# Words to convert on ScalarE's DMA queue, and other wire times in the scheduler of the first stage

## The chip, the cores and the metric

The kernel runs on one core of a Trainium2 chip. A core has five engines with queues of their own: TensorE (PE, matmuls), VectorE (DVE), ScalarE (ACT), GpSimd (POOL) and SyncE (SP), which here only issues DMAs. ACT and POOL can issue DMAs too. The metric is the device time of one execution in microseconds; 1666.36 us is the median of three runs before the change.

## The reference

Attention over keys and values that are averaged over groups of eight, and behind it two layers of two matrix products each. Shapes: 8 batches, 8 heads, 576 positions, head size 64; both layers go from 512 to 2048 and back over 4608 tokens.

```
k_p = k.reshape(B, H, Sp, 8, D).mean(axis=3)         # Sp = 72, v alike
scores = scale * np.matmul(q, k_p.transpose(0, 1, 3, 2))
attn = softmax(scores)                                # minus the row maximum
x = np.matmul(attn, v_p) ...reshape(4608, 512)
h = np.maximum(x @ w_in, 0.0);   x = (h * h) @ w_out  # first layer
h = x @ w_in2;  return np.maximum(0.01 * h, h) @ w_out2
```

The four weight matrices reach the core as 8-byte floats; the kernel converts them itself.

## The kernel before

Products of 4-byte floats are made of two rounded parts: a high and a low part of each operand, and three matmuls (high by high, high by low, low by high). The work falls into stages. The first, up to about 591 us, holds the attention and the first matrix product of layer one; the middle one forms the second product of layer one from seven products of quarter matrices (class `Middle`, matmuls L1752); the last does layer two (L1970, L2213).

**The first stage.** Tokens go in nine blocks of 512. For each block: q is loaded (L212) and turned, scored against pooled keys (L749), made to probabilities (ACT L771), turned again (L829, L837), split to `pth`, `ptl`, `ptr` (ACT L843, DVE L846) and multiplied with values (L890 to L893), giving `xh` and `xl` (L902, L906). Units of 12 matmuls follow (L1021), squared after a relu (ACT L1032, L1035) and stored by POOL's queue (L1051). For each batch the K rows (L176, 1024 KB into `wo4`) and a tail of 64 rows (L163, into `raw`) are pooled by DVE (L507, L589), and the V rows (L183, 1024 KB into `wo5`) with a remainder of six loads of 32 rows (L193, into `wo2`).

**Conversions.** In the same stage 38 jobs convert the weights that later stages need. A job's words (512 KB, in one or two DMAs, L346, into `wo0` or `wo1`) are loaded; ACT takes the exponent (L243), DVE puts the bits together (L247 to L264, L1535), and POOL's queue stores the parts into `w1o`, `w2i`, `w2o`.

**The order.** The first 117 us are written out by hand. From there `FirstStage` adds every operation to a `Plan` with an engine, an estimated duration, a rank, what it comes after and which buffers it takes. `Plan.run` picks whichever can start first by its own account, ties by rank, and emits instructions in that order: an engine's program is what the account made of it, and the engine executes it in order. The account has a `wire` for loads: each transfer that has a wire time lengthens it, an SP operation isn't planned before `wire - QUEUED`, and what reads the data is planned no sooner than `lag` behind the issue, or the end of the wire and 2.0. SP's account runs 15 us (`AHEAD`) ahead of the others.

**The stage's end.** `add_second_stage` (L1596) loads weights of the middle stage from `w1o`: eight `wo` tiles (384 KB) and eight `wi` tiles (512 KB), L1719. Loads of `wo0`, `wo1`, `wo3` come after everything of attention and conversion; `wi4` to `wi7` come after units of the last block, whose weight buffers they take. ACT and DVE split each (L1725, L1727), and TensorE starts with `wo0`.

Of the kernel before, what the change touches and what calls it, by code (L numbers as in the profile page):

```python
# [16 lines left out]
P = 128  # L17
POOL = 8
# [25 lines left out]
def attention_relu2_leaky_kernel(  # L44
# [12 lines left out]
    nc = tc.nc  # L57
# [3 lines left out]
    SP = S // POOL  # L61
    PAIR = 2 * SP
    NP = H // 2
    KEYS = H * SP
# [79 lines left out]
    def load_to(key, fn, tag, shape=(P, 512)):  # L144
        t = sb(list(shape), F32, tag)
        fn(t)
        raws[key] = t
# [11 lines left out]
    def k_load(b, c):  # L159
        n = min(P, KEYS - c * P)  # L160

        def fn(t):
            nc.sync.dma_start(out=t[:n], in_=rows_of(k, b)[c * P : c * P + n])  # L163

        return fn
# [145 lines left out]
    class Weights:  # L311
# [5 lines left out]
        def load(self, n):  # L317
            self.steps[n][0]()
# [10 lines left out]
    class Stored:  # L329
# [8 lines left out]
            self.steps = self.run(range(self.at, end), val, sums)  # L338
            self.at = end

        def load(self, h, t=None):
            w, kind, _, i, n = self.jobs[h]
            if t is None:
                t = sb([P, 512, 2], U32, "val")
            for src, to in half_words_of(w, kind, i, n):
                nc.sync.dma_start(out=to(t), in_=src)  # L346
            return t[:, :, 0], t[:, :, 1]

        def run(self, jobs, val_tag, sums_tag):
# [843 lines left out]
    class Plan:  # L1193
# [1 line left out]


        SLACK = {"PE": 1.5, "ACT": 0.3, "DVE": 0.3, "SP": 0.3, "POOL": 0.3}
        AHEAD, QUEUED = 15.0, 5.0

        def __init__(self, counts):  # L1200
            self.ops, self.counts, self.rings, self.wire = [], counts, {}, -self.AHEAD
# [70 lines left out]
    class FirstStage:  # L1272

        STORED, VALUES, CHAIN, POOLING, SUMS, UNITS = 9, 0, 1, 3, 4, 6
        STORED_AT, STORED_EVERY = 30.0, 10.5

        def __init__(self):
            counts = {"ps": 4, "acc": 4, "pt": 1, "prem": 3, "x0": 1, "x1": 1, "placed": 1}
# [9 lines left out]
            self.last.append(x)  # L1288
            return x

        def dma(self, fn, rank, kb, n=1, rate=260.0, **k):
            return self.op("SP", 0.35 * n, fn, rank, lag=4.0, wire=kb / rate, **k)

        def out(self, fn, rank, kb, n=1, **k):
            return self.op("POOL", 0.8 * n, fn, rank, lag=6.0, wire=kb / 350.0, **k)

        def add_keys(self, b, rank):
            rows, tail, kp, km, kl, kt = (
                Buffer(t) for t in ("wo4", "raw", "kp", "gh", "km", "kt")
            )  # L1300
            load = self.dma(
                lambda: load_to(("k", b, "rows"), k_load_all(b), "wo4", (P, 4, 512)),
                rank, 1024, gets=[rows])
            load_tail = self.dma(
                lambda: load_to(("k", b, "tail"), k_load(b, KEYS // P), "raw"), rank, 128, gets=[tail])
            steps = []
            x = load
            for n, us in enumerate((1.22, 0.69, 0.43)):
                def fn(n=n):
                    if n == 0:  # L1310
                        steps.extend(k_pool_rows(b))
                    steps[n]()
                after = [x, self.scored.get(b - 2)] if n == 0 else [x]
                x = self.op("DVE", us, fn, rank, after=after, gets=[kp] if n == 0 else (), uses=[rows, kp])
            y = self.op("DVE", 1.03, lambda: k_pool_tail(b), rank, after=[load_tail, x], uses=[tail, kp])
            masks = []

            def mask(n):
                if n == 0:
                    masks.extend(k_mask_parts(b))  # L1320
                masks[n]()

            x = self.op("DVE", 0.68, lambda: mask(0), rank, after=[x, y], gets=[km, kl], uses=[kp])
            y = self.op("DVE", 0.28, lambda: mask(1), rank, after=[x, y], uses=[kp, kl])
            parts = []

            def turn(n):
                if n == 0:
                    parts.extend(k_transpose_parts(b))
                parts[n]()  # L1330

            p0, p1 = Buffer("ps"), Buffer("ps")
            t0 = self.op("PE", 0.63, lambda: turn(0), rank, after=[x, y], gets=[p0, kt], uses=[km])
            c0 = self.op("DVE", 0.69, lambda: turn(1), self.CHAIN, after=[t0], uses=[p0, kt])
            t1 = self.op("PE", 0.2, lambda: turn(2), rank, after=[y, t0], gets=[p1], uses=[kl])
            c1 = self.op("DVE", 0.22, lambda: turn(3), self.CHAIN, after=[t1, c0], uses=[p1, kt])
            self.keys[b] = [c0, c1], kt

        def add_v(self, b, rank):
            rows, rem, vp, vr, vh, rh = (  # L1340
                Buffer(t) for t in ("wo5", "wo2", "vp", "vr", "vh", "rh")
            )
            x = self.dma(
                lambda: load_to(("v", b, "rows"), v_load_all(b), "wo5", (P, 4, 512)),
                rank, 1024, gets=[rows])
            y = self.dma(
                lambda: load_to(("rem", b, "rows"), rem_load_all(b), "wo2", (P, 2, 512)),
                rank, 384, n=6, gets=[rem])
            steps = {}

            def pool(what, n):
                if n == 0:
                    steps[what] = (v_pool_rows if what == "v" else rem_pool_rows)(b)
                steps[what][n]()

            for n, us in enumerate((1.22, 0.69, 0.43)):
                x = self.op("DVE", us, lambda n=n: pool("v", n), rank, after=[x],
                            gets=[vp] if n == 0 else (), uses=[rows, vp])
            for n, us in enumerate((0.69, 0.42, 0.29)):
                y = self.op("DVE", us, lambda n=n: pool("r", n), rank, after=[y],  # L1360
                            gets=[vr] if n == 0 else (), uses=[rem, vr])

            def split(n):
                if n == 0:
                    steps["s"] = v_split_parts(b)
                steps["s"][n]()

            a = self.op("DVE", 0.72, lambda: split(0), rank, after=[x, y], gets=[vh, rh], uses=[vp])
            c = self.op("DVE", 0.5, lambda: split(1), rank, after=[a], uses=[vr, rh])
            c = self.op("DVE", 0.63, lambda: split(2), rank, after=[c], uses=[vr, rh])  # L1370
            self.vs[b] = [a, c], [vp, vr, vh]
# [23 lines left out]
        def add_attention(self, blk):  # L1395
# [3 lines left out]
            tiles = list(range(t0 // P, (t0 + T) // P))  # L1399
# [5 lines left out]
            for i in tiles:  # L1405
                for b, *_ in parts_of(i):
                    if b not in keyed:
# [1 line left out]
                        self.add_keys(b, self.POOLING)  # L1409
                two = len(parts_of(i)) - 1  # L1410
                raw, qt, ps = Buffer("raw"), Buffer("qt"), Buffer("ps")
                x = self.dma(lambda i=i: load_to(("q", i), q_load(i), "raw"), self.POOLING, 256,
                             n=1 + two, rate=130.0, gets=[raw])
                qp = q_transpose_parts(i)

                def copy(i=i, fn=qp[1]):
# [57 lines left out]
        def add_unit(self, blk, c, n):  # L1474
# [16 lines left out]
            x = self.plan.op("ACT", 0.6, powers, self.VALUES, after=[x], gets=[r], uses=[acc])  # L1491
            x = self.plan.op("ACT", 0.63, lambda: square(at["r"]), 2, after=[x], uses=[r])
            steps = store_parts(blk, c, lambda: at["r"], nc.gpsimd)
            y = self.plan.op("POOL", 0.8, steps[0], 0, after=[x], uses=[r], lag=4.0, wire=0.73)
            if len(steps) > 1:
                total = Buffer("gh" if blk else "wo3")
                x = self.plan.op("DVE", 0.69 if blk else 0.42, steps[1], self.SUMS,
                                 after=[x, self.even], gets=[total], uses=[r, self.even_r])
                self.plan.op("POOL", 0.8, steps[2], 0, after=[x], uses=[total], lag=4.0, wire=0.73)
            self.even, self.even_r = y, r  # L1500

        def add_stored(self, jobs):
            words, before = {}, None
            for h in jobs:
# [7 lines left out]
                def run(fn, st=st):  # L1512
                    return lambda: fn(st)

                def load(st, h=h, i=i, n=n, tiles=tiles):
                    if n == 0:
                        tiles[0] = sb([P, 2, 512, 2], U32, f"wo{i % 2}")
                    st["low"], st["top"] = stored.load(h, tiles[0][:, n])

                first = x = self.dma(run(load), R, 512, n=1 + kind, gets=[val] if n == 0 else (),  # L1520
                             uses=[val], behind=first if n else None)
                x.ready = self.STORED_AT + h * self.STORED_EVERY
                x = self.op("ACT", 0.67, run(lambda st: exponent(st["top"])), R, after=[x], uses=[val])

# [13 lines left out]
                to = forms[name][i]  # L1538
                if kind == 0 and n == 0:
                    y = self.out(run(lambda st, to=to: stored.first_half(st["o"], to, nc.gpsimd)()),  # L1540
                                 R, 128, after=[x], uses=[gl])
                    before = st, gl, x
                    continue
                sums, steps = Buffer("wo3"), []
# [10 lines left out]

                more = [] if kind else [before[1]]
                after = [x] if kind else [x, before[2]]
                x = self.out(run(begin), R, 192 if kind else 256, n=2, after=after, uses=[gl, *more])
                x = self.op("DVE", 1.0 if kind else 0.84, step, R, behind=x, gets=[sums], uses=[gl, *more])
                if not kind:  # L1560
                    x = self.op("DVE", 0.84, step, R, after=[x], uses=[sums, gl, *more])
                y = self.out(step, R, 256 if kind else 512, after=[x], uses=[sums])
            self.stored_last = y

        def run(self):
# [763 lines left out]
```

## Time and profile before

| | us |
|---|---|
| median of three runs (1665.43 to 1667.23) | 1666.36 |
| the profiled execution | 1666.54 |
| its span on the core | 1664.8 |
| PE busy in it | 1617.9 (97%) |
| DVE busy | 1268.0 (76%) |
| ACT busy | 835.2 (50%) |
| POOL busy | 170.5 (10%) |

An engine's busy time is what its instructions cover; issuing DMAs is not counted. A wait is the idle time of an engine just before an instruction, with what released it. The granted clock of TensorE (PEclk) is a share of its full speed; half of it is 1.2 GHz. DMA share is the mean busy share of 16 DMA engines.

### The profile page before, as it was taken

What the parts mean: (1) busy time and instruction counts of PE and PEld (TensorE: products, weight loads), DVE (VectorE), ACT (ScalarE), POOL (GpSimd) and SP (SyncE); (2) the same over time, 40 slices, a digit from 0 to 9 for tenths busy, and PEclk for the clock granted to TensorE, in tenths of its full rate; (3) what the DMA queues carried; (4) which work ended last, traced back from release to release, by engine and by line L of the source; (5) the groups of instructions that cost most, each with busy time, mean ns of one, the idle gap of its engine ahead of it and who ended that gap; (6) DMA issues with size and microseconds to landing.
All of it is one profiled execution on the core that took longest, in us unless ns stands there. A gap on an engine that the chain in (4) does not pass through costs nothing. (4 is left out here: it accounts for less than half of the span.)

```text
span 1664.8 us, 26658 instructions
## 1 busy us (share of the span) xinstructions
PE 1617.9 (97%) x9560; PEld 1471.1 (88%) x9560; DVE 1268.0 (76%) x2214; ACT 835.2 (50%) x1797; POOL 170.5 (10%) x289
## 2 busy tenths in 40 slices
PE   7997998999999999999999999999999999999998
PEld 6886787788888888888888899999999999999998
DVE  7986697888775578786968978877877876666665
ACT  6764576666755654443435544443445533333332
POOL 0111322233334310000000000000000000000000
PEclk9999999999999999999999999999999999999999
DMA  8846577676557877575757856556638754444443
GB/s 233 272 147 185 187 230 211 203 233 231 202 208 248 286 252 260 184 259 189 252 186 258 290 201 231 176 197 226 197 139 291 234 180 156 154 158 152 152 155 105
DMA packets 249700, 345.78 MB, mean 208 GB/s; under 512 B 55360, under 2 KB 175168, under 8 KB 249568
## 3 DMA queue, kind: packets, MB, share of 16 engines
q1 hardware_dynamic: 228704, 278.92, 52.2%
q0 software_dynamic: 20288, 64.64, 10.6%
q8 instruction: 75, 1.23, 0.3%
q10 hardware_dynamic: 576, 0.52, 0.1%
q14 instruction: 57, 0.47, 0.1%
HBM read 208.74 MB, written 135.27 MB: 207 GB/s over the span
## 5 line engine op out<-in xcount | busy, mean ns | idle before, releaser
L1021 PE MATMUL acc<-xh,wi 128*128 128x512 f32 x640 | 219.0, 400 | 0.0
L1021 PE MATMUL acc<-wo,wi 128*128 128x512 f32 x704 | 197.3, 407 | 5.5 <-ACT r L1032 5.4
L1021 PEld LDWEIGHTS acc<-wo,wi 128*128 128x128 f32 x704 | 132.4, 193 | 32.7 <-ACT r L1032 6.8
L1021 PEld LDWEIGHTS acc<-xh,wi 128*128 128x128 f32 x640 | 120.2, 188 | 23.8 <-ACT wi L303 0.2
L1021 PE MATMUL acc<-xl,wi 128*128 128x512 f32 x320 | 125.1, 391 | 0.0
L2213 PE MATMUL ps<-wi,hh 128*128 128x256 f32 x512 | 93.9, 283 | 0.0
L2213 PE MATMUL acc<-wi,hh 128*128 128x256 f32 x496 | 91.1, 283 | 0.0
L2213 PE MATMUL ps<-wo,hh 128*128 128x256 f32 x496 | 90.9, 283 | 0.0
L2213 PE MATMUL acc<-wo,hh 128*128 128x256 f32 x484 | 88.8, 283 | 0.0
L1707 ACT CAST mh<-ms 128x512 fp32r<-128x512 f32 (+2 forms) x68 | 52.4, 771 | 72.2 <-DVE ms L1689 72.0
L771 ACT ACTIVATE s<-ps,m 128x72 f32<-128x72 f32 x240 | 73.8, 330 | 29.4 <-DVE m L759 29.3
L1970 PE MATMUL acc<-fh,wo 128*128 128x384 f32 x384 | 82.9, 338 | 2.7 <-DVE gh L1983 1.6
L1970 PE MATMUL ps<-fh,wi 128*128 128x384 f32 x384 | 82.3, 336 | 0.2 <-DVE gh L1983 0.2
L1986 ACT ACTIVATE gh<-gh 128x384 f32<-128x384 f32 x48 | 25.3, 527 | 112.0 <-DVE gh L1983 112.0
L2213 PEld LDWEIGHTS ps<-wi,hh 128*128 128x128 f32 x512 | 79.9, 192 | 0.0
L2213 PEld LDWEIGHTS acc<-wi,hh 128*128 128x128 f32 x496 | 77.4, 192 | 0.0
L2213 PEld LDWEIGHTS ps<-wo,hh 128*128 128x128 f32 x496 | 77.4, 192 | 0.0
L1752 PE MATMUL acc<-mh,wi 128*128 128x512 f32 (+1 forms) x256 | 76.0, 363 | 0.0
L1752 PE MATMUL ps<-mh,wi 128*128 128x512 f32 (+1 forms) x256 | 76.0, 363 | 0.0
L2213 PEld LDWEIGHTS acc<-wo,hh 128*128 128x128 f32 x484 | 75.5, 192 | 0.0
L1032 ACT ACTIVATE r<-acc 128x512 f32<-128x512 f32 x88 | 52.5, 604 | 44.0 <-PE acc L1021 42.6
L2213 PE MATMUL ps<-wi,hl 128*128 128x256 f32 x256 | 72.4, 283 | 0.0
(359 smaller groups left out, 4518.0 us busy)
## 6 DMA issues: line engine op xcount, KB each, us to landing
h<-r POOLq DMA_DIRECT2D x88, 256.0 KB, 3.7
hf<-r SPq DMA_DIRECT2D x96, 192.0 KB
ml<-h SPq DMA_DIRECT2D x34, 512.0 KB
ml<-h SPq DMA_DIRECT2D x60, 256.0 KB
hr<-hf SPq DMA_DIRECT2D x23, 640.0 KB
xl<-hf SPq DMA_DIRECT2D x23, 640.0 KB
xh<-hf SPq DMA_DIRECT2D x23, 640.0 KB
h<-st POOLq DMA_DIRECT2D x56, 256.0 KB, 4.0
```

What stands on the lines that cost most here:

```text
L771: nc.scalar.activation(out=s[:, g, :], in_=at["ps"][:, h * SP : (h + 1) * SP], func=AF.Exp, bias=m[:, g : g + 1], accum_out=l[:, g : g + 1],)
L1021: nc.tensor.matmul(acc_of[blk, c], lhsT=(wih, wil)[w][c][:, kc], rhs=xsplit[blk][x][kc], start=(kc, n) == order[0], stop=(kc, n) == order[-1],
L1032: nc.scalar.activation(out=r, in_=ps, func=AF.Relu)
L1707: nc.scalar.copy(hi[:, at], y)
L1752: nc.tensor.matmul(at[s][:, :n], lhsT=w[:, wx, b, s * P : (s + 1) * P], rhs=x[:, a], start=p == 0 and m == 0, stop=p == PAIRS - 1 and m == 2,)
L1970: nc.tensor.matmul(at, lhsT=w[:, FORMS[j], kc], rhs=x[j][:, kc], start=m == 0 and j not in (4, 6), stop=m == 5, skip_group_check=True,)
L1986: nc.scalar.activation(out=out_, in_=x, func=AF.Lrelu)
L2213: nc.tensor.matmul(at[:, s * TR : (s + 1) * TR], lhsT=x[:, a, s * P : (s + 1) * P], rhs=w[:, b], start=p == 0 and s == 0 and m == 0, stop= ...
```

## The change

Word loads of the planned stage are issued by ACT, with a lag of 10 and no wire. Loads that stay on SP have wire times of their own, longer than before for each kind: K and V rows 5.0 (3.9 before, 1024 KB over 260), a K tail 1.5 (0.5), a V remainder 4.0 (1.5), q 4.8 (2.0). `QUEUED` doubles. Stores by POOL have a lag of 7 and no wire. The word loads of the last stage, which have no plan, stay on SP.

```
-        def load(self, h, t=None):
+        def load(self, h, t=None, queue=nc.sync):
...
-                nc.sync.dma_start(out=to(t), in_=src)
+                queue.dma_start(out=to(t), in_=src)
...
-        AHEAD, QUEUED = 15.0, 5.0
+        AHEAD, QUEUED = 15.0, 10.0
...
+        ROWS, TAIL, REST, QUERY = 5.0, 1.5, 4.0, 4.8
...
-        def dma(self, fn, rank, kb, n=1, rate=260.0, **k):
-            return self.op("SP", 0.35 * n, fn, rank, lag=4.0, wire=kb / rate, **k)
-
-        def out(self, fn, rank, kb, n=1, **k):
-            return self.op("POOL", 0.8 * n, fn, rank, lag=6.0, wire=kb / 350.0, **k)
+        def dma(self, fn, rank, wire, n=1, **k):
+            return self.op("SP", 0.35 * n, fn, rank, lag=4.0, wire=wire, **k)
+
+        def out(self, fn, rank, n=1, **k):
+            return self.op("POOL", 0.8 * n, fn, rank, lag=7.0, **k)
...
-                rank, 384, n=6, gets=[rem])
+                rank, self.REST, n=6, gets=[rem])
...
-            y = self.plan.op("POOL", 0.8, steps[0], 0, after=[x], uses=[r], lag=4.0, wire=0.73)
+            y = self.plan.op("POOL", 0.8, steps[0], 0, after=[x], uses=[r], lag=4.0)
...
-                first = x = self.dma(run(load), R, 512, n=1 + kind, gets=[val] if n == 0 else (),
-                             uses=[val], behind=first if n else None)
+                    st["low"], st["top"] = stored.load(h, tiles[0][:, n], nc.scalar)
+
+                first = x = self.op("ACT", 0.35 * (1 + kind), run(load), R, lag=10.0,
+                                    gets=[val] if n == 0 else (), uses=[val], behind=first if n else None)
```

Lines behind the first added constant stand one lower in the changed kernel (L1719 is L1720 there).

Below are SP's rows of the kernel before for the V load of block 3 (`wo5_1533`, its remainder `wo2_1566`), issued at 150.77 us, with the words of the first conversion `wo0_1459` behind it. DMAHW0 to DMAHW7 are the completion semaphores of hardware DMAs, in turn.

```order
L183 DMA wo5_1533<-in_v 128x4x512 [waits DVE_49]
L193 DMA wo2_1566<-in_v 32x1x512 [waits DMAHW7_49,DVE_49]
L193 DMA wo2_1566<-in_v 32x1x512 [waits DMAHW0_49]
L193 DMA wo2_1566<-in_v 32x1x512 [waits DMAHW1_49]
L193 DMA wo2_1566<-in_v 32x1x512 [waits DMAHW2_49]
L193 DMA wo2_1566<-in_v 32x1x512 [waits DMAHW3_49]
L193 DMA wo2_1566<-in_v 32x1x512 [waits DMAHW4_49]
L346 DMA wo0_1459<-in_moe_w_out 128x2x256 [waits DMAHW5_49]
L346 DMA wo0_1459<-in_moe_w_out 128x2x256 [waits DMAHW6_49]
L212 DMA raw_1642<-in_q 128x8x64 [waits DMAHW7_49,PE_49]
```

In the changed kernel the same words (`wo0_1454` there) stand among ACT's instructions:

```order
L1035 ACTIVATE r_1524<-r_1524 128x512 [waits Activation_49]
L712 COPY qt_1562<-ps_1548 128x512 [waits PE_49]
L346 DMA wo0_1454<-in_moe_w_out 128x2x256 [waits DMAHW4_49]
L346 DMA wo0_1454<-in_moe_w_out 128x2x256 [waits DMAHW6_49]
L1032 ACTIVATE r_1580<-acc1_1423 128x512 [waits DMASW6_49,PE_49]
```

They left the place behind the remainder in SP's queue for one between an ACT copy and an ACT relu.

For block 5 the changed SP queue has these rows from the V load on:

```order
L183 DMA wo5_2937<-in_v 128x4x512 [waits DVE_49]
L193 DMA wo2_2958<-in_v 32x1x512 [waits DMAHW7_49,DMAHW0_49,DVE_49]
L193 DMA wo2_2958<-in_v 32x1x512 [waits DMAHW0_49]
L193 DMA wo2_2958<-in_v 32x1x512 [waits DMAHW1_49]
L193 DMA wo2_2958<-in_v 32x1x512 [waits DMAHW2_49]
L193 DMA wo2_2958<-in_v 32x1x512 [waits DMAHW3_49]
L193 DMA wo2_2958<-in_v 32x1x512 [waits DMAHW4_49]
L163 DMA raw_3020<-in_k 64x512 [waits DMAHW5_49,PE_49]
```

and ACT, at the same place of the program, these:

```order
L346 DMA wo1_3041<-in_moe_w_out 128x2x256 [waits DMAHW6_49]
L346 DMA wo1_3041<-in_moe_w_out 128x2x256 [waits DMAHW7_49]
L346 DMA wo1_3041<-in_moe_w_out 128x2x256 [waits DMAHW0_49]
L346 DMA wo1_3041<-in_moe_w_out 128x2x256 [waits DMAHW1_49]
L843 CAST ptr_3013<-ps_3045 96x2x128 [waits PE_49]
```

The four words wait for the completions of the V rows (DMAHW6) and of the first three pieces of the remainder.

At the stage's end SP has, before:

```order
L1719 DMA wo0_5866<-w1o_73 128x768 [waits DMAHW5_49,DVE_49]
L1719 DMA wo1_5873<-w1o_73 128x768 [waits DMAHW6_49]
L1719 DMA wo3_5878<-w1o_73 128x768 [waits DMASW4_49,DMASW5_49,DMASW3_49,DMASW6_49,DMASW2_49,DMASW7_49,DMASW1_49,DMAHW7_49,DMASW0_49,DVE_49]
L1719 DMA wi3_5883<-w1o_73 128x1024 [waits DMAHW0_49,PE_49]
...
L1719 DMA wi6_6026<-w1o_73 128x1024 [waits DMAHW5_49,PE_49]
L1719 DMA wi7_6058<-w1o_73 128x1024 [waits DMAHW6_49,PE_49]
```

and in the changed kernel:

```order
L1720 DMA wi5_5965<-w1o_73 128x1024 [waits DMAHW1_49,DMASW1_49,PE_49]
L1720 DMA wi6_6014<-w1o_73 128x1024 [waits DMAHW2_49,DMASW7_49,PE_49]
L1720 DMA wi7_6050<-w1o_73 128x1024 [waits DMAHW3_49,PE_49]
L1720 DMA wo0_6057<-w1o_73 128x768 [waits DMAHW4_49,DVE_49]
L1720 DMA wo1_6060<-w1o_73 128x768 [waits DMAHW5_49]
L1720 DMA wo3_6062<-w1o_73 128x768 [waits DMASW5_49,DMASW6_49,DMASW4_49,DMASW7_49,DMASW3_49,DMAHW6_49,DMASW2_49,DVE_49]
```

The three `wo` loads moved from ahead of `wi3` to behind `wi7`, which waits for TensorE.

## Rows read from the trace of the kernel before

**Rows 1.** Waits of PE, 115 to 620 us: sum, times, longest.

```profile
PE ps L893 <- DVE ptr L846: 5.6, 1, 5.6
PE acc L1021 <- ACT r L1032: 5.4, 1, 5.4
PE ps L837 <- DVE ptl L846: 4.4, 1, 4.4
PE ps L829 <- DVE ptr L846: 3.8, 1, 3.8
PE ps L1752 <- ACT mh L1707: 2.8, 1, 2.8
```

**Rows 2.** Windows after each of those: length, five engines' busy time, PEclk, DMA share, GB/s.

```profile
133.38:140.00 6.62, 6.62 (x27) 6.07 (x28) 4.37 (x10) 4.62 (x22) 0.54 (x1) 0.64 0.58 185
...
169.49:178.00 8.51, 8.41 (x25) 6.58 (x26) 6.40 (x14) 4.75 (x10) 3.78 (x6) 0.64 0.92 303
...
261.97:270.00 8.03, 8.03 (x32) 7.03 (x33) 7.53 (x20) 5.88 (x28) 3.12 (x5) 0.64 0.60 190
...
304.77:312.00 7.23, 7.16 (x33) 5.96 (x34) 6.94 (x16) 4.21 (x20) 1.81 (x3) 0.76 0.39 121
...
600.54:608.00 7.46, 7.12 (x44) 6.92 (x45) 6.21 (x13) 3.21 (x7) 0.00 (x0) 0.77 0.64 217
```

**Rows 3.** Timeline of DVE and ACT: start, length, instruction, idle before it.

```profile
131.64 1.23 DVE L507 TENSOR_TENSOR wo<-wo 128x1024 f32<-128x1024 f32 x1 [8.29 <-DMA wo<-in_k]
...
168.30 0.65 ACT L243 ACTIVATE wo<-wo 128x512 f32<-128x512 f32 x1 [5.87 <-DMA wo<-in_moe_w_out]
...
260.19 1.00 DVE L589 TENSOR_REDUCE kp<-raw 64x64 f32<-64x512 f32 x1 [6.83 <-DMA raw<-in_k]
...
303.26 1.00 DVE L589 TENSOR_REDUCE kp<-raw 64x64 f32<-64x512 f32 x1 [5.81 <-DMA raw<-in_k]
```

**Rows 4.** Timeline of SP's DMA issues: start, time the issues took.

```profile
117.95 0.38 SPq L176 DMA_DIRECT2D wo<-in_k  x1
118.60 9.76 SPq L212 DMA_DIRECT2D raw<-in_q  x2
...
150.77 0.37 SPq L183 DMA_DIRECT2D wo<-in_v  x1
...
157.05 1.25 SPq L346 DMA_DIRECT2D wo<-in_moe_w_out  x2
...
161.69 8.18 SPq L346 DMA_DIRECT2D wo<-in_moe_w_out  x4
...
245.99 0.53 SPq L163 DMA_DIRECT2D raw<-in_k  x1
...
284.24 0.37 SPq L183 DMA_DIRECT2D wo<-in_v  x1
...
291.75 0.75 SPq L163 DMA_DIRECT2D raw<-in_k  x1
```

**Rows 5.** A window inside the second stall, columns as in rows 2.

```profile
166.00:168.00 2.00, 0.00 (x0) 0.00 (x0) 0.00 (x0) 0.00 (x0) 0.79 (x1) 1.00 0.14 44
```

**Rows 6.** Issues of L346 (115 to 620) and L2255: min/median/max ns, first and last.

```profile
L346 SPq DMA_DIRECT2D wo<-in_moe_w_out x44: 540/612/6154, 135.2 to 522.4; - x44
...
L2255 ACTq DMA_DIRECT2D out<-r x2: 372/374/376, 1657.3 to 1660.0; - x2
```

**Rows 7.** Waits of ACT, 115 to 620 us: the first row.

```profile
ACT r L1032 <- PE acc L1021: 37.0, 34, 3.0
```

**Rows 8.** The stage's end: SP's issues, ACT, and a window as in rows 2.

```profile
568.66 1.67 SPq L1719 DMA_DIRECT2D wo<-w1o  x3
...
577.00 14.60 SPq L1719 DMA_DIRECT2D wi<-w1o  x4
...
596.73 1.05 ACT L1725 CAST wi<-wi 128x1024 fp32r<-128x1024 f32 x1 [2.71 <-DMA wi<-w1o]
...
590.00:600.00 10.00, 7.72 (x60) 7.32 (x58) 6.75 (x10) 5.57 (x10) 2.27 (x5) 1.00 0.96 320
```

More of the change, by code (lines that the diff above doesn't have):

```diff
@@ L1302, in add_keys @@
                 lambda: load_to(("k", b, "rows"), k_load_all(b), "wo4", (P, 4, 512)),
-                rank, 1024, gets=[rows])
+                rank, self.ROWS, gets=[rows])
             load_tail = self.dma(
-                lambda: load_to(("k", b, "tail"), k_load(b, KEYS // P), "raw"), rank, 128, gets=[tail])
+                lambda: load_to(("k", b, "tail"), k_load(b, KEYS // P), "raw"), rank, self.TAIL, gets=[tail])
             steps = []
@@ L1344, in add_v @@
                 lambda: load_to(("v", b, "rows"), v_load_all(b), "wo5", (P, 4, 512)),
-                rank, 1024, gets=[rows])
+                rank, self.ROWS, gets=[rows])
             y = self.dma(
                 lambda: load_to(("rem", b, "rows"), rem_load_all(b), "wo2", (P, 2, 512)),
-                rank, 384, n=6, gets=[rem])
+                rank, self.REST, n=6, gets=[rem])
             steps = {}
@@ L1411, in add_attention @@
                 raw, qt, ps = Buffer("raw"), Buffer("qt"), Buffer("ps")
-                x = self.dma(lambda i=i: load_to(("q", i), q_load(i), "raw"), self.POOLING, 256,
-                             n=1 + two, rate=130.0, gets=[raw])
+                x = self.dma(lambda i=i: load_to(("q", i), q_load(i), "raw"), self.POOLING, self.QUERY,
+                             n=1 + two, gets=[raw])
                 qp = q_transpose_parts(i)
@@ L1498, in add_unit @@
                                  after=[x, self.even], gets=[total], uses=[r, self.even_r])
-                self.plan.op("POOL", 0.8, steps[2], 0, after=[x], uses=[total], lag=4.0, wire=0.73)
+                self.plan.op("POOL", 0.8, steps[2], 0, after=[x], uses=[total], lag=4.0)
             self.even, self.even_r = y, r
@@ L1517, in load @@
                         tiles[0] = sb([P, 2, 512, 2], U32, f"wo{i % 2}")
-                    st["low"], st["top"] = stored.load(h, tiles[0][:, n])
-                first = x = self.dma(run(load), R, 512, n=1 + kind, gets=[val] if n == 0 else (),
-                             uses=[val], behind=first if n else None)
+                    st["low"], st["top"] = stored.load(h, tiles[0][:, n], nc.scalar)
+                first = x = self.op("ACT", 0.35 * (1 + kind), run(load), R, lag=10.0,
+                                    gets=[val] if n == 0 else (), uses=[val], behind=first if n else None)
                 x.ready = self.STORED_AT + h * self.STORED_EVERY
@@ L1540, in add_stored @@
                     y = self.out(run(lambda st, to=to: stored.first_half(st["o"], to, nc.gpsimd)()),
-                                 R, 128, after=[x], uses=[gl])
+                                 R, after=[x], uses=[gl])
                     before = st, gl, x
@@ L1557, in add_stored @@
                 after = [x] if kind else [x, before[2]]
-                x = self.out(run(begin), R, 192 if kind else 256, n=2, after=after, uses=[gl, *more])
+                x = self.out(run(begin), R, n=2, after=after, uses=[gl, *more])
                 x = self.op("DVE", 1.0 if kind else 0.84, step, R, behind=x, gets=[sums], uses=[gl, *more])
@@ L1561, in add_stored @@
                     x = self.op("DVE", 0.84, step, R, after=[x], uses=[sums, gl, *more])
-                y = self.out(step, R, 256 if kind else 512, after=[x], uses=[sums])
+                y = self.out(step, R, after=[x], uses=[sums])
             self.stored_last = y
```

## The prediction

> **What bounds the kernel now.** I read the waits of TensorE (PE) first. After the start there are four long ones and one middling one up to 620 us [rows 1]: 5.6, 5.4, 4.4 and 3.8 us behind VectorE (DVE) or ScalarE (ACT), and 2.8 behind the `mh` of the stage that follows; the rows below them in that view are 1 us or less. TensorE is otherwise never short of work, so only what feeds it at these places can move the time. The second view is the granted clock from the moment work resumes after each of the five [rows 2]: full speed is 1.00, and 0.64, 0.64, 0.64, 0.76 and 0.77 stand there, mixtures of the half level (1.2 GHz) with the full one (2.4). One minus the clock, times the length, is time lost to it: 0.36x6.62 + 0.36x8.51 + 0.36x8.03 + 0.24x7.23 = 2.4+3.1+2.9+1.7 = 10.1 us for the first four, 0.23x7.46 = 1.7 for the fifth. So the first four sites cost 19.2 us idle and 10.1 at a low clock, **29.3 us**.
>
> The third view says what the releaser itself was waiting for [rows 3]. None computes late; each sits before a transfer: DVE 8.29 us on K rows, ACT 5.87 on words to convert, DVE 6.83 and 5.81 on a K tail. The fourth is SyncE's issues (SP) [rows 4]. K rows issued at 117.95 are used at 131.64, 13.7 us later. Words issued from 157.05 came at 168.30, some 11. The K tails of 245.99 and 291.75 came at 260.19 and 303.26: 14.2 and 11.5. In each case V rows and the six short loads of the V remainder went out just ahead. From the issue of the V rows to the landing of what stands behind the remainder it was 17.5 us (150.77 to 168.30) and 19.0 (284.24 to 303.26). While that queue drains the DMA share is 0.14 [rows 5], which is 2.2 of 16 engines: the remainder keeps two engines busy and the rest have run dry. SyncE itself is also held: two loads of q took 9.76 us to issue and four words 8.18, against a median of 0.61 for one of words [rows 4, 6].
>
> **The change, part by part.** (1) The 60 word transfers of the stage leave SyncE for ScalarE's queue and are emitted 10 us, by the plan, ahead of their conversion. (2) K rows, V rows, remainder, tails and q are given longer wire times, so consumers are planned later or loads earlier. (3) Stores cost no wire. The counts of computing instructions don't change; what counts is where loads stand. I count lead as TensorE work standing between an issue and its first use in the two orders, each matmul at the spacing of its kind in the trace; such a lead is an estimate.
>
> - Site 1. K rows had 7.6 us of lead and get 23.4; they needed 13.7. The wait goes.
> - Site 2. The words had 5.6 and 2.9 us and get 11.4 to 12.6, on a queue with no remainder ahead of them. They go too, if ScalarE's queue is not slowed by the remainder (rivals).
> - Sites 3 and 4. The K tails had 5.2 and 4.9 us; the two that follow a remainder get 12.4 and 12.9. Counted from the V rows, these uses stand at +17.2 and +17.8, and landings come at +17.5 to +19.0. So 0 to 2 us of DVE wait stay, less what its backlog hides. I take 1.0 for the first (bounds 0 and 5, the second being the 4.4 of site 3 and a little clock), and 1.5 for the other.
>
> All four removed: -29.3 us, and +2.5 for what of 3 and 4 stays.
>
> What is added on ScalarE is 60 issues. Its own DMA issues show only at the end of the run, at 0.37 us; SyncE's of the same words have a median of 0.61 and a maximum of 6.2 [rows 6]. At 0.37 to 0.61 the 60 are 22 to 37 us of ScalarE over 470 us. What hides them is its own waits for TensorE: the longest sort alone is 37 us there [rows 7]. Where that cover is gone a store of `r` or a probability tile is later by one issue. I take 1.0 us, bounds 0 and 6 (one word issue in ten, 0.61 each, on TensorE's path, and one held for 2 us).
>
> An issue on ScalarE can also be held. Hardware transfers carry eight completion names in turn (DMAHW0 to 7 in the order), whichever engine issues, and each waits for the transfer eight before. In the changed order four words of block 5's stretch follow right behind V rows, remainder and tail, so ScalarE waits at the first for the V rows and then for the first three pieces of the remainder. By TensorE work the V rows are 5.1 us old there and the third piece 5.8. With 5.4 for the 512 KB of `wi7` (below) I put the end of V rows and first pieces at 6 to 9, an estimate. ScalarE stands 1 to 4 us, with casts of `pth` and `ptr` queued behind, which TensorE needs. I take 1.0 us of TensorE here (0 to 4) and 0.7 at block 6's like place (0 to 4).
>
> The end of the stage gets worse. Before, `wo0`, `wo1` and `wo3` were issued at 568.66, 22 us ahead of need, and `wi4` to `wi7` after them; TensorE found them split when the first stage ended, about 591.3, when `wi7`, the last of the four issues from 577.00, could go [rows 8]. In the changed order `wi5`, `wi6` and `wi7` stand ahead of `wo0`, and `wi7` waits for the stage's last matmuls, which use the buffer. So `wo0` goes out at T+0.2, T being the end of the stage, behind 512 KB. `wi7` came at 596.73, 5.4 us; 384 KB more at the 320 GB/s of that stretch is 1.2, and 0.4 for its issue. ScalarE's cast is 0.8 (768 columns, by its 1.05 for 1024), and DVE's low half, about as long, costs 0.6 past the first two products, which need the cast alone. TensorE stands 0.2+5.4+1.6+0.8+0.6 = 8.6 us, and 0.5 more for `wo3` later, in place of 2.8: +6.3. The clock after it I put at the 2.4 of site 1, against 1.7: +0.7. Sum **+7.0**. Bounds: +4 if `wo0` lands with `wi7` (their pieces run on different engines at the same time), +10 if it is as slow as `wi7`, 4.1 for 384 KB.
>
> The profiled execution took 1666.5 us (span 1664.8 and 1.7 around it), 0.2 over the median. Sum: 1666.5 - 29.3 + 2.5 + 1.0 + 1.7 + 7.0 = 1649.4, so **1649**.
>
> **A rule weighed.** In the drains two engines work [rows 5] while SyncE's later loads wait. The Trainium skill (DMA: Bandwidth & Descriptors, "Issuing engines are not separate DMA queues") says that transfers started by any engine run on the same 16 DMA engines and interleave, and that a second issuer saves only sequencer time; by that rule two sixteenths of the words still stand behind the remainder, and the sum would be D's below, 1658. The same page ("Queues, rings and completion order") says each DMA engine turns in rotation between the rings it has work for; by that, words in ScalarE's own ring pass the backlog on those two engines, and the sum stands. No run of before has words on ScalarE's queue, so both stay open.
>
> **The rivals.**
> (A) All landings are in time and ScalarE's issues are hidden: only the boundary at its lower bound is left, 1666.5-29.3+4 = 1641. For it: all K rows and most words gain 5 to 16 us of lead. Against: +17.2 and +17.8 meet landings of 17.5 to 19.0.
> (B) The tails behind the remainder come as late as ever: two sites persist at their full size, 4.4+2.9+3.8+1.7 = 12.8 in place of the 2.5. 1649.4+10.3 = 1660. For it: nothing makes the remainder drain faster. Against: 12 us of lead where there were 5.
> (C) Slower: ScalarE is held at its word issues as SyncE was, 5.6 to 9 us at a time [rows 4], since the ring or the completion names make it wait, and it stands in front of every activation, cast and copy of the stage. Four such sites, of the old size with the clock behind them, give back 29.3: 1649.4-4.2+29.3 = 1674. It decides from about 6 us per site, idle and clock together, which is 4 us of idle. For it: 8.18 us for four word issues; ScalarE has more dependants than SyncE. Against: words come every 10 us and hang behind a remainder at two or three places only.
> (D) The words land as late by ScalarE's queue and site 2 stays (5.4+3.1): 1658. It lies in the range.
>
> **How the numbers follow.** Forecast 1649 (1644 to 1655): 0.50. A: 0.15. B and D together: 0.22. C, and anything else that ends slower: 0.13. A measurement of this kernel can tell about 0.2% from no change, 3.3 us: 1663 to 1669.7 is the same. B's upper part gives 0.05 of it and C's lower part 0.02. Faster 0.82, same 0.07, slower 0.11. The range reaches from A's upper half to B and a little beyond: 1639 to 1664.
>
> **What would show it.** In the profile of the changed kernel the idles of L893, L837 and L829 behind `ptr` and `ptl` and the one of L1021 behind `r` should be under 2 us each, with full granted clock from 120 to 590. DVE should no longer wait for `in_k` rows, and for tails 2 us at most. ACT's waits for `in_moe_w_out` should be gone; word issues should last 0.4 to 0.6 us, with 1 to 4 us at block 5's. At the boundary TensorE should show its largest idle of the run after the start, 7 to 10 us, on `wo`, and half clock behind it. Wrong would be: ACT issues of over 4 us at several places (C), tails waited for over 4 us (B), or no idle at the boundary.

## The result: 1645.6 us, and where the time came from

The changed kernel takes 1645.58 us (median of four runs, 1643.97 to 1647.16) against 1666.8 in the same series: a ratio of 0.9869, 95% interval 0.9848 to 0.9890. The forecast was 1649, range 1639 to 1664. The profiled execution took 1644.27 us, its span is 1642.2.

TensorE's waits in the stage, answering to [rows 1]:

```profile
PE ps L1753 <- ACT wo L1726: 8.5, 1, 8.5
PE ps L837 <- DVE ptl L846: 0.7, 1, 0.7
PE ps L749 <- DVE wo L906: 0.5, 1, 0.5
PE ps L829 <- DVE ptr L846: 0.3, 1, 0.3
PE ps L1753 <- DVE wo L1728: 0.2, 1, 0.2
```

The four long waits are gone and one of 8.5 us is new, at the first matmul of the middle stage. Windows, columns as in [rows 2]; the first is the stage up to 540 us, the second the new idle, the third what follows it:

```profile
120.00:540.00 420.00, 418.06 (x2149) 349.94 (x2148) 325.91 (x754) 282.19 (x854) 143.68 (x239) 1.00 0.70 229
...
561.90:570.60 8.70, 0.18 (x2) 0.00 (x1) 2.73 (x5) 3.28 (x5) 2.17 (x4) 0.70 1.02 400
570.60:580.00 9.40, 9.20 (x57) 8.91 (x58) 6.96 (x11) 4.19 (x7) 0.00 (x0) 0.73 0.64 219
```

TensorE is idle 1.9 of 420 us with the clock granted in full; behind the boundary 0.27x9.40 = 2.5 us go to the clock. What of the queues? SyncE's issues, answering to [rows 4], and below them the tail of 223.03 where DVE uses it, as in [rows 3]:

```profile
123.54 5.47 SPq L176 DMA_DIRECT2D wo<-in_k  x1
...
215.46 0.37 SPq L183 DMA_DIRECT2D wo<-in_v  x1
215.94 4.00 SPq L193 DMA_DIRECT2D wo<-in_v  x6
...
223.03 7.55 SPq L163 DMA_DIRECT2D raw<-in_k  x1
...
235.42 1.08 DVE L589 TENSOR_REDUCE kp<-raw 64x64 f32<-64x512 f32 x1 [1.10 <-DMA raw<-in_k]
```

Nothing there has become faster. From the V rows (215.46) to the tail's landing (235.42) it is 20.0 us, no less than the 17.5 and 19.0 of before, and SP is held 7.55 us at the tail and 5.47 at K rows. The uses stand later instead: DVE waits 1.1 us for a tail in the whole stage, once, and no wait of TensorE follows from it.

The word issues, now ACT's (min/median/max ns), answering to [rows 6], and ACT at block 5's four words, where the order made it wait for the V rows' and the remainder's completions:

```profile
L346 ACTq DMA_DIRECT2D wo<-in_moe_w_out x44: 547/606/917, 136.4 to 511.0; - x44
L346 ACTq DMA_DIRECT2D wo<-in_moe_w_in x16: 374/374/519, 325.3 to 463.8; - x16
```

```profile
265.36 4.41 ACTq L346 DMA_DIRECT2D wo<-in_moe_w_out  x3
269.81 0.37 ACT L843 CAST ptr<-ps 96x256 fp32r<-96x256 f32 x1 [3.90 <-PE ps L837]
```

No issue is held over 0.92 us. ACT stood 3.9 us there; the row names PE as the releaser, but what ends just before 269.81 is the last of ACT's own issues. The trace's records of completions bear that out: the third and the fourth of the words go out at 267.45 and 269.22, each 0.02 us after a piece of the remainder is complete. No wait of TensorE follows from it.

At block 6 the same happens at one word issue, which goes out 0.02 us after the second piece of the remainder is complete (332.07). ACT stands 6.0 us there, and PE is again named in its place:

```profile
332.09 0.39 ACTq L346 DMA_DIRECT2D wo<-in_moe_w_in  x1
332.52 0.32 ACT L902 CAST wo<-ps 128x192 fp32r<-128x192 f32 x1 [6.01 <-PE ps L837]
```

DVE waits 5.4 us for that cast, and the waits of 0.5, 0.7 and 0.3 us in the list above follow at 333.28, 336.15 and 337.59. So this stand cost TensorE 1.5 us.

The stage's end, answering to [rows 8], with the last store of a conversion (L432) first:

```profile
559.93 0.76 POOL L432 DMA_DIRECT2D w2o<-wo  x1 [0.21 <-DVE ml L1712]
...
547.83 14.60 SPq L1720 DMA_DIRECT2D wi<-w1o  x4
562.52 3.87 SPq L1720 DMA_DIRECT2D wo<-w1o  x3
...
569.72 1.77 ACT L1726 CAST wo<-wo 128x768 fp32r<-128x768 f32 x2 [4.86 <-DMA wo<-w1o]
...
570.60 0.58 PE L1753 MATMUL ps<-mh,wo 128*128 128x256 f32 x1 [8.52 <-ACT wo L1726]
```

`wo0` to `wo3` go out behind `wi7` at 562.5, the first landed at 569.7, and TensorE, done with the stage at 562.1 (570.60 less 8.52), starts at 570.6. Before, the last such store was 27 us ahead of the stage's end; now it is 2 us ahead:

```profile
563.55 0.76 POOL L432 DMA_DIRECT2D w2o<-wo  x1
```

### The profile page after: what moved, and what is told of

It reads as the page before. It is cut to its first block, busy times and chain, and to the rows that moved or that the text cites. A ratio compares the mean times of both kernels' runs of the same rounds, so it can differ in the third digit from the quotient of the medians.

```text
span 1642.2 us, 26646 instructions
## 1 busy us (share of the span) xinstructions
PE 1608.6 (98%) x9560; PEld 1463.3 (89%) x9560; DVE 1265.7 (77%) x2214; ACT 836.6 (51%) x1797; POOL 170.9 (10%) x289
## 5 line engine op out<-in xcount | busy, mean ns | idle before, releaser
L1021 PE MATMUL acc<-xh,wi 128*128 128x512 f32 x640 | 219.5, 401 | 0.0
L1021 PE MATMUL acc<-wo,wi 128*128 128x512 f32 x704 | 190.5, 398 | 0.0
L1021 PEld LDWEIGHTS acc<-wo,wi 128*128 128x128 f32 x704 | 129.3, 188 | 25.3 <-issue 0.4
L1021 PEld LDWEIGHTS acc<-xh,wi 128*128 128x128 f32 x640 | 120.1, 188 | 24.0 <-ACT r L1032 0.5
L1021 PE MATMUL acc<-xl,wi 128*128 128x512 f32 x320 | 124.9, 390 | 0.0
L1753 PE MATMUL ps<-mh,wo 128*128 128x512 f32 (+1 forms) x224 | 68.3, 366 | 8.7 <-ACT wo L1726 8.5
```

What stands on the lines that cost most here:

```text
L1021: nc.tensor.matmul(acc_of[blk, c], lhsT=(wih, wil)[w][c][:, kc], rhs=xsplit[blk][x][kc], start=(kc, n) == order[0], stop=(kc, n) == order[-1],
L1753: nc.tensor.matmul(at[s][:, :n], lhsT=w[:, wx, b, s * P : (s + 1) * P], rhs=x[:, a], start=p == 0 and m == 0, stop=p == PAIRS - 1 and m == 2,)
```

## Experiments

The theory to test: a stall stands where the lead of a load (TensorE's work between its issue and its use) is shorter than the drain behind a V remainder (the time until the remainder and what queued behind it are in), whatever the queue; the plan's account sets the leads. The rivals: ScalarE's queue itself makes the words and everything else faster; or the order is a lucky one.

**The queue without the wire times.** The kernel before with the two edits that move the words (below), and nothing else.

```
+                queue.dma_start(out=to(t), in_=src)          # nc.scalar
+                first = x = self.op("ACT", 0.35 * (1 + kind), run(load), R, lag=10.0, ...)
```

> Words on ScalarE's queue with the old wire times. In this order the K rows of site 1 keep 7.6 us of lead, all words get 8 to 15, one tail that stalled stands ahead of its V rows now, and wo0 to wo3 keep their place ahead of wi4. Theory (a stall stands where a load's lead is shorter than the drain behind the remainder): only site 1 stays (5.6 idle and 2.4 of clock) and the end of the stage costs its old 2.8: 1666.5-29.3+8.0 = 1645 to 1648, PE waiting some 5 us at L893 for ptr. Rival 1 (the queue removes the words' stall alone): 1666.5-8.5 = 1658. Rival 2 (the queue takes everything away since SP is free): 1637.

1649.51 us, ratio 0.9890 (0.9873 to 0.9906). TensorE's waits, then SP and DVE at site 1:

```profile
PE ps L893 <- DVE ptr L846: 5.6, 1, 5.6
PE ps L1752 <- ACT mh L1707: 3.9, 1, 3.9
```

```profile
120.01 0.38 SPq L176 DMA_DIRECT2D wo<-in_k  x1
...
133.68 1.22 DVE L507 TENSOR_TENSOR wo<-wo 128x1024 f32<-128x1024 f32 x1 [8.27 <-DMA wo<-in_k]
```

The time is 1.5 us above the expected 1645 to 1648, and the waits are as the theory had them: the one load whose lead is as short as before stalls as before, 13.7 us after its issue again. The tails, whose places the new order moved, make DVE wait 1.8 us, once. That the words left SP did nothing for the K rows. This edit also takes the words out of the account of SP's wire, so it alone doesn't say whether the queue or the plan removed the other stalls; the third run bears on that.

**The wire times without the queue.** The changed kernel, words loaded from SP and with their old wire time.

```
-                first = x = self.op("ACT", 0.35 * (1 + kind), run(load), R, lag=10.0, ...)
+                first = x = self.dma(run(load), R, 512 / 260.0, n=1 + kind, ...)
```

> New wire times, QUEUED 10, stores without wire; words stay on SP with their old wire time (512 KB over 260). Theory: the K leads are as long as in the changed kernel and the words' leads are 5 to 27 us with none just behind a remainder, so the four stalls go here too and the end of the stage has its 8.5 us idle: 1644 to 1650. Rival (words need ScalarE's queue): a stall at L243 of 5 us or more with its clock, 1653 or more.

1659.66 us, ratio 0.9955 (0.9939 to 0.9972): the time missed, at the other end of the stage.

```profile
PE ps L1753 <- ACT wo L1726: 13.6, 1, 13.6
PE ps L1753 <- DVE wo L1728: 4.8, 1, 4.8
PE ps L1753 <- ACT mh L1708: 3.5, 1, 3.5
```

```profile
549.57 11.20 SPq L1720 DMA_DIRECT2D wi<-w1o  x4
569.41 14.92 SPq L1720 DMA_DIRECT2D wo<-w1o  x3
...
579.17 0.76 POOL L432 DMA_DIRECT2D w2o<-wo  x1 [3.63 <-DVE wo L430]
```

The four stalls are gone on SP's queue as well; 21.9 us of idle stand at the boundary to the middle stage. With the longer account the words, which still count in it, are planned late: the last store of a conversion is at 579.17, some 18 us after the last `wi` load went out at the end of the stage (549.57 and 11.20). On SP `wo0` waits 8.6 us for DVE's last addition of a conversion and `wo3` 13.6 us for stores, that one last. I had looked at the leads and not at when the conversions end.

**The changed plan, words issued by SP.** The plan still books an ACT operation with a lag of 10; the issuing instruction is SP's. SP gets to them a little earlier (the first at 133.1 for 136.4 us).

```
-                    st["low"], st["top"] = stored.load(h, tiles[0][:, n], nc.scalar)
+                    st["low"], st["top"] = stored.load(h, tiles[0][:, n])
```

> The plan of the changed kernel, each word load issued by SP at the place where ACT issues it. Only the queue differs. Theory: K tails and words of block 5 share SP's queue behind the remainder; words issued there have 10 to 13 us of lead and need about 14 from the tail on, so one site stalls 2 to 5 us and the sum is 1646 to 1654. Rival (two queues share the same DMA engines, so the queue is no matter): within 2 us of the changed kernel, 1645. ACT's stand of 4 us at its issues of block 5 goes in both.

1644.90 us, ratio 0.9866 (0.9851 to 0.9881): the rival was right, the queue makes no difference to the time.

```profile
PE ps L1753 <- ACT wo L1726: 8.4, 1, 8.4
PE ps L703 <- DMA raw<-in_q: 1.5, 1, 1.5
PE ps L749 <- DVE ptr L846: 1.2, 1, 1.2
```

```profile
L346 SPq DMA_DIRECT2D wo<-in_moe_w_out x44: 540/620/2988, 133.1 to 502.9; - x44
...
  ACT wo L243: 6.2, 4
```

ACT waits 6.2 us for words, four times, TensorE 1.0 to 1.5 at three places, and the total is the same within 0.7 us. What the change needed was for the words to be outside the account of SP's wire and 10 us ahead (which of the two wasn't separated); who issues them makes no difference to the time here. The Trainium skill's rule weighed in the prediction (DMA: Bandwidth & Descriptors, "Issuing engines are not separate DMA queues") has the DMAs of any engine run on the same 16 DMA engines and interleave, and a second issuer save only sequencer time. In the time this run agrees with it; site 2 did not stay, though, as rival D would have had it, since lead had replaced the place in the queue.

The landing does depend on the queue. By the traces' records of completions the first of block 5's words took 7.8 us from ACT's queue (264.74 to 272.49) and was complete before two pieces of the remainder that SP had issued 3 us earlier (274.34 and 277.51). From SP's queue it took 11.2 us (265.94 to 277.16) and was complete behind the last piece (275.65). So words in a queue of their own do pass part of the backlog; with 10 us of lead TensorE doesn't need that.

**The remainder on more engines, in the kernel before.** Each load of 32 rows cut in two of 16, twelve for six; the plan as before.

```
-                    nc.sync.dma_start(
-                        out=t[2 * REM * n : 2 * REM * (n + 1), c],
-                        in_=rows[2 * c : 2 * c + 2, P:, :],
-                    )
+                    for j in range(2):
+                        r0 = REM * (2 * n + j)
+                        nc.sync.dma_start(out=t[r0 : r0 + REM, c], in_=rows[2 * c + j, P:, :])
```

> The kernel before with each load of 32 remainder rows cut in two of 16 rows (12 instead of 6 loads per batch), so that a load's rows can go to 16 engines. Nothing else differs. Theory (the stalls are the drain of two engines): the remainder is gone in 3 us, the four waits go or fall below 1 us each with the old queue and the old wire times, the end of the stage stays as before: 1666.5-29.3+1 = 1636 to 1642. Rival (the time is SP's issuing, 12 issues now for 6): waits stay or grow, 1663 to 1672.

1645.44 us, ratio 0.9868 (0.9853 to 0.9883).

```profile
PE ps L1751 <- ACT mh L1706: 3.5, 1, 3.5
PE acc L1020 <- ACT r L1031: 2.4, 2, 1.6
PE ps L892 <- DVE ptr L845: 1.6, 1, 1.6
PE acc L1751 <- DVE ml L1710: 1.4, 1, 1.4
PE ps L828 <- DVE ptl L845: 1.0, 1, 1.0
```

SP and DVE at site 1, then a window just ahead of the landing, columns as in [rows 2]:

```profile
121.96 0.39 SPq L176 DMA_DIRECT2D wo<-in_k  x1
...
128.76 1.23 DVE L506 TENSOR_TENSOR wo<-wo 128x1024 f32<-128x1024 f32 x1 [4.26 <-DMA wo<-in_k]
...
124.00:128.00 4.00, 4.00 (x19) 3.06 (x18) 0.50 (x1) 0.37 (x1) 0.00 (x0) 1.00 0.91 273
```

This is the cause by itself: with the old queue, the old account and the old leads the K rows come 6.8 us after their issue instead of 13.7, and the stalls shrink to 1.6 us and less. Part of the 6.8 is that SP is longer at the twelve issues, so that the K rows go out later; counted from the V rows they come after 14.6 us instead of 18.7.

The traces' records of completions show how. A load's completion is recorded in 16 parts, a remainder load of 32 rows in two at its end. In the kernel before, 14 parts of the K rows were complete by 124.34, the last two at 131.42 and 131.62; DVE started at 131.64. Of the K tail issued at 245.99, 14 parts were complete by 248.65 and the last two at 259.40 and 260.16. So a whole load waits for its shares on the two DMA engines that the remainder has put behind. The planned loads of 16 rows complete in 16 parts each, and all parts of the K rows behind them come between 127.37 and 128.74.

The edit is worth as much as the whole change. It came out a little above the 1636 to 1642 expected: the waits left up to 620 us are 9.9 us together, 4.9 of them in the middle stage, which had 3.1 before.

**The stage's end.** Three kernels try to take the 8.5 us away. In the first, `wo0` and `wo1` come after the last DVE addition of a conversion instead of after its store, and are issued ahead of `wi4` again.

```
-                        after = both if p in (0, 1, 3) else attention
+                        after = (words_free if p < 2 else both) if p in (0, 1, 3) else attention
```

> The changed kernel, where wo0 and wo1 of the middle stage come after the last DVE addition of a conversion (when the words' buffers are free) instead of after the last store; in the order they stand ahead of wi4 again, wo3 stays behind wi7. Theory (the 8.5 us idle at the stage's end is wo0 behind wi7): that idle goes; wo3 lands about 8 us after the end of the stage and is needed after some 6.6, so 2 to 3 us of idle at the fourth group: 1645.5-8.7-2.4+2.5+1 = 1637 to 1640. Rival (the idle is the transfer rate at the boundary, not the order): 1643 or more.

1645.81 us, ratio 0.9867 (0.9849 to 0.9885), where 1637 to 1640 was expected: no gain. The idle moved from the first group of the middle stage to the fourth:

```profile
571.03 0.32 SPq L1721 DMA_DIRECT2D wo<-w1o  x1
571.40 0.45 SPq L1676 DMA_DIRECT2D xl<-h  x1
...
579.77 0.58 PE L1754 MATMUL ps<-mh,wo 128*128 128x256 f32 x1 [8.95 <-ACT mh L1709]
```

`wo3` could not be issued before 571.03, since its buffer was still being stored from (the last store went out at 567.45), and the loads of that group's tokens (`xl`, `xh`) stand behind it on SP. The order of `wo0` and `wi7` had been only half of it. The conversions' end is the other: in the second kernel they are planned 10.0 us apart instead of 10.5.

```
-        STORED_AT, STORED_EVERY = 30.0, 10.5
+        STORED_AT, STORED_EVERY = 30.0, 10.0
```

> The changed kernel with STORED_EVERY 10.0 instead of 10.5: conversions end some 14 us earlier in the plan, and wo0, wo1 and wo3 stand ahead of wi6. Theory: boundary idle falls to the 2.8 to 4 that the kernel before and the one with the queue alone have; the rest of the stage, in a new order, stays without waits over 2 us: 1638 to 1642. Rival (any new order brings stalls of its own, the gain was luck of one order): 1648 or more.

1642.28 us, ratio 0.9848 (0.9833 to 0.9863), just above what was expected.

```profile
PE ps L749 <- ACT s L771: 2.1, 1, 2.1
PE ps L1753 <- ACT mh L1708: 1.2, 1, 1.2
PE ps L1753 <- DVE wo L1728: 1.0, 1, 1.0
```

```profile
236.71 1.07 DVE L589 TENSOR_REDUCE kp<-raw 64x64 f32<-64x512 f32 x1 [4.07 <-DMA raw<-in_k]
...
549.10 0.76 POOL L432 DMA_DIRECT2D w2o<-wo  x1 [0.53 <-DVE wo L430]
```

The last store is at 549.10, 11 us earlier, and the boundary idle falls from 8.7 to 2.5 us (a third row has 0.3). Only half of that arrives: in the new order there are waits of 2.1 us and less within the stage again. The longest, at 240.75, stands behind 4.1 us that DVE waits for a K tail behind a remainder (the last two of its 16 parts came 10 and 12 us after the others), and the clock is 0.61 over the 4.25 us that follow. The next, 0.7 us at 260.56, stands behind 6.1 us in which ACT waited at word issues. So the stalls of the sites come back, smaller, when the order moves the uses. The third kernel has both edits.

> Both of the two edits: wo0 and wo1 ahead of wi2, wo3 ahead of wi6. Theory: nothing but the wi7 load is late at the boundary, 2 to 3 us: 1636 to 1640, within 2 us of the better of the two. Rival (the shift of conversions brings a stall): 1645 or more.

1643.49 us, ratio 0.9855 (0.9838 to 0.9873): no better than the second alone, and above the 1636 to 1640 expected; its longest boundary wait is 3.0 us.

**The remainder on more engines, in the changed kernel.** With `wo0` and `wo1` early first:

> wo0 and wo1 early, and the remainder in twelve loads of 16 rows. Theory: the changed plan has no stall left that the remainder causes, so this adds nothing: within 2 us of the one with wo0 and wo1 early alone, 1637 to 1640. Rival (waits of 1 to 2 us for tails and q still cost): 2 to 4 us less, 1634 to 1636. Against both: twelve issues of 0.4 to 0.6 us keep SP longer and q comes late, 1642 or more.

1641.42 us, ratio 0.9841 (0.9823 to 0.9859), with 9.3 us still idle on `mh` at the fourth group. Against 1645.81 without the cut remainder it is 4 us less, which I had given to a rival; the time itself is above both forecasts, 1637 to 1640 and 1634 to 1636. Then the cut alone:

> The changed kernel with the remainder in twelve loads of 16 rows, nothing else. Theory: the changed plan keeps its uses behind the drain already and has only 1.9 us of small waits from 120 us to the end of the stage; the boundary idle stays 8 to 9 us: 1643 to 1645, the same as the changed kernel. Rival (drains still cost in it by tails and q, or by ACT's stand of 4 us): 1640 or less.

1640.51 us, ratio 0.9839 (0.9825 to 0.9853); the rival again, to half a microsecond. The stage up to 540 us, and SP at the V load that stands above for the changed kernel:

```profile
120.00:540.00 420.00, 420.00 (x2166) 353.43 (x2165) 328.29 (x758) 285.06 (x855) 143.14 (x239) 1.00 0.71 232
```

```profile
215.07 0.37 SPq L183 DMA_DIRECT2D wo<-in_v  x1
215.54 8.04 SPq L195 DMA_DIRECT2D wo<-in_v  x12
...
224.16 0.70 SPq L163 DMA_DIRECT2D raw<-in_k  x1
```

SP is no longer held (0.70 for the tail, 7.55 above), and TensorE has no idle time at all in 420 us; the 1.5 us behind ACT's stand at block 6 are gone too. That is 1.9 of the 5 us. The stage ends 4 us earlier (558.0 for 562.1); 0.4 of it is idle time before 120 us, and the 1.7 left are not idle time of TensorE and stay open. Last, the cut together with conversions every 10.0 us:

> The changed kernel with the remainder in twelve loads of 16 rows and STORED_EVERY 10.0. Theory (at the stage's end the wait is for the last conversion, and the plan's other small waits are the remainder): both go, boundary 2 to 3 us, other waits of the stage under 2 together: 1636 to 1640, the fastest. Rival (the new order of STORED_EVERY 10.0 brings waits of 3 to 4 us that have nothing to do with the remainder): 1641 to 1643.

1640.23 us, ratio 0.9835 (0.9821 to 0.9849), the lowest median, but not to be told from the cut alone (runs from 1636.64 to 1640.38, and 1639.71 to 1641.28). Its boundary waits are 2.5, 1.0 and 0.3 us where the other has 8.8, and of the waits that 10.0 alone brought into the stage only 0.2 us is left: they too were the remainder's. The profile is that of its fastest run, 1636.64 against 1640.00 for the profile of the cut alone; why the gain doesn't show in the median stays open.

## Why the prediction was right, point by point

- **The four sites, -29.3.** Right: all four waits and the low clock behind them are gone, as leads against the needed 13.7, 11 and 14 us said. Shown by three runs that separate lead, queue and drain. The whole span bears it out: it is 22.6 us shorter, of which TensorE's busy time gives 9.3 (1617.9 to 1608.6, the same work at a higher clock) and its idle time 13.3.
- **Sites 3 and 4 keep 2.5.** Mis-sized. The tail did land 20.0 us after its V rows, later than the 19.0 taken, and DVE did wait: 1.1 us, once. TensorE's cost was none: it ran unit matmuls (L1021) meanwhile. The step that failed is the one that took a DVE wait for a TensorE wait. The landings of 17.5 to 19.0 were also read from two sites only: at site 3 it had been 22.8 us (237.37 to 260.19), with words between V rows and remainder, so a longer wait stood in the trace of before.
- **ScalarE's issues 1.0, and its stand at block 5 and 6, 1.7.** At block 5 the stand came where the completion names put it and as long as forecast (3.9 us, 1 to 4), and cost TensorE nothing. At block 6 it was 6.0 us, longer than forecast, and cost 1.5, where 0.7 was taken. That the two terms together (1.7) are near the 1.5 measured is luck. The 1.0 for the other issues doesn't show.
- **The end of the stage, +7.0.** The idle is 8.7 us against 8.6 forecast for its first part, in place of the 2.8 of [rows 1] and 0.3 behind it: +5.6; the clock takes 2.5, not 1.7: +0.8. So +6.4. The mechanism was incomplete: `wi7` was in front, but `wo3` waited for the last store as well, and moving `wo0` alone gave nothing.
- **The sum.** The stage's other waits are 1.7 us in all, the 1.5 at block 6 among them, and were 1.8 before, so on balance the small terms come to nothing. That makes 1666.5 - 29.3 + 6.4 = 1643.6, against 1644.3 profiled; the 0.7 between them I can't place. The forecast of 1649.4 was too high by the 5.2 us of small terms and 0.6 at the stage's end.
- **What I credited wrongly.** Site 2 was put down partly to a queue without a remainder ahead of it. The run with the same plan and the words on SP shows that the queue isn't needed. Rival C, ScalarE held like SyncE at four sites, is refuted by issues of 0.92 us at most and by 1.5 us of TensorE behind its two stands; B by the tails.

## What to carry to other kernels

Where a consumer waits for a load, compare the lead at the issue with the time to its landing behind whatever stands ahead on the same DMA engines: the plan's account of the slowest small transfer decided more here than which engine issues. Before rewriting the account, reshape that transfer: twelve loads of 16 rows for six of 32 gave as much as the whole change. An engine that computes and also issues can stand at an issue behind another queue's slow transfer, 6.0 us here. And when loads are pushed about, look at what becomes last: here the end of the conversions, which gave back 6 us of 29 in the change and 22 of idle in its half.

## What was not expected of the hardware

SyncE was held at single issues for 5.47 and 7.55 us in the changed kernel, as in the one before; with the remainder in twelve loads the tail of the same place took 0.70 to issue. That doesn't hold everywhere: in the kernel before with twelve loads, the tail behind the K rows of site 1 was still held 5.9 us. ScalarE's issues were never held over 0.92 us in the changed kernel (1.85 in the one with the queue alone), and the same words on either queue gave the same time within 0.7 us. Nor was it expected that 14 of 16 parts of a load are there 7 us (K rows of site 1) or 11 us (K tail of site 3) before the last two.
